# Deferring part of P V into the next scores phase, and a new ending, in a decode attention kernel that streams its K and V caches

## The chip, the cores and the metric

One core of one Trainium2 chip runs the whole program. The metric is the device time of that core in microseconds (us), the median of several executions.

## The reference

```python
# B=4 sequences, one query each, H=32 heads, Sk=8192 cached keys, Dh=128, D=512, bf16
xn = layernorm(x)
q = (xn @ wq)                                   # (B, H, 1, Dh)
scores = einsum("bhqd,bhkd->bhqk", q, k_cache) * Dh**-0.5
o = einsum("bhqk,bhkd->bhqd", softmax(scores), v_cache)
out = x + o.reshape(B, 1, H*Dh) @ wo + ffn(xn)  # ffn: silu gate, up, down; small
```

The K and V caches are 268 MB each. Nothing of them is used twice, so the kernel is a stream of loads with matrix work beside it.

## The kernel before

The work is cut into 32 tiles of 4 heads of one sequence. A tile's K is 8.39 MB, its V as much, and three slots of that size hold them in SBUF. The scores phase is 32 pieces: DVE transposes a piece of K (`kt`), PE multiplies it with q (`sps`). After the softmax, P V is 64 chunks of PE (`oacc`), one tile later. All loads go through one queue of the sync engine.

```python
    def load_v(n, parts=(T,)):                  # T = 256 columns of Dh
        t_ = slot()
        ...
            nc.sync.dma_start(out=t_[:, c0:c1], in_=src[:, c0:c1])
    ...
    def t_piece(n, g, jb):                      # DVE: one transpose of 128 x 512 uint32
        ...
        nc.vector.transpose(out=kt[:]..., in_=src[:, :, jb, :])
    def s_piece(n, g, jb):                      # PE: two matmuls
        ...
    build_q(0)
    load_v(0)
    for i in range(NT):                         # NT = 32
        for g in range(NTG):                    # 16 groups of 2 pieces
            for jb in range(2):
                t_piece(i, g, jb)
                s_piece(i, g, jb)
            if g == 1 and i > 0:
                pt_turn(i - 1)                  # four DVE transposes of P
        ...                                     # load_v(i), wo and parts near the end
        max_1(i)
        if i + 1 < NT:
            build_q(i + 1)
        ...
        for k in range(NK):                     # NK = 64
            pv_chunk(i - 1, k)
            if k == 8:
                max_2(i)
        row_sums(i)
        ...
        elif i + 2 < NT:
            load_k(i + 2)                       # K, two tiles ahead
        if bv == B - 1:
            fin_1(jv)                           # closing of a group of four tiles
            fin_q(jv)
    n = NT - 1
    pt_turn(n)
    wo_some(H)
    for k in range(KM):                         # half of the last tile as chunks
        pv_chunk(n, k)
    fin_1(JL)
    xps = x_tile()
    pv_last(xps, KM * NV, T - 48, start=True)   # the rest with V stationary
    fin_2(JL, xps)
    pv_last(xps, T - 48, T)
```

## Time and profile before

| | before |
|---|---|
| time, median of 3 runs | 1304.74 us |
| span of the profiled run | 1305.5 us |
| bytes read | 550.77 MB |
| mean rate over the span | 422 GB/s |
| PE busy in the middle (110 to 1180 us) | 88 to 89% |

The prediction below shows the slices, the stretches and the waits. Three more lines of the page of the kernel before are needed later. A DMA ring here means one of the core's 16 DMA engines with the packets that wait for it. The first two lines are instruction fetches, by queue (packets, MB, share of the 16 rings' time); as shown further down, they move over the same rings as the data. The third is the chain that ended last, by share of the span.

```profile
q8 instruction: 37, 0.61, 0.2%
q14 instruction: 21, 0.17, 0.0%
...
PE 58%; DVE 20%; issue 18%; DMA 2%; ACT 0%; DVEq 0%; SPq 0%
```

The chain is compute: PE, DVE and their handing over make 96% of it. The fetches look like nothing: 0.78 MB of 551. I passed over them when I predicted.

### The profile page before, as it was taken

What the parts mean: (1) busy time and instruction counts of PE and PEld (TensorE: products, weight loads), DVE (VectorE), ACT (ScalarE), POOL (GpSimd) and SP (SyncE); (2) the same over time, 40 slices, a digit from 0 to 9 for tenths busy, and PEclk for the clock granted to TensorE, in tenths of its full rate; (3) what the DMA queues carried; (4) which work ended last, traced back from release to release, by engine and by line L of the source; (5) the groups of instructions that cost most, each with busy time, mean ns of one, the idle gap of its engine ahead of it and who ended that gap; (6) DMA issues with size and microseconds to landing.
All of it is one profiled execution on the core that took longest, in us unless ns stands there. A gap on an engine that the chain in (4) does not pass through costs nothing.

```text
span 1305.5 us, 12271 instructions
## 1 busy us (share of the span) xinstructions
PE 1136.1 (87%) x4725; PEld 463.8 (36%) x4788; DVE 807.9 (62%) x1509; ACT 35.0 (3%) x79; POOL 3.6 (0%) x11
## 2 busy tenths in 40 slices
PE   1898888988889988889988889988889988889889
PEld 0244333333333333333333333333333333333335
DVE  3956555676555676555676555686555776555771
ACT  1000000000000000000000000000000000000000
POOL 1000000000000000000000000000000000000000
PEclk9897999889989899899998899988999889989899
DMA  9999999999999999999999999999999999999985
GB/s 418 418 432 438 432 432 436 428 442 420 446 422 442 428 436 430 436 430 434 432 436 427 428 424 438 424 432 432 414 436 432 430 428 424 436 436 406 409 339 227
DMA packets 12466, 551.56 MB, mean 422 GB/s; under 512 B 1260, under 2 KB 1784, under 8 KB 3064
## 3 DMA queue, kind: packets, MB, share of 16 engines
q1 hardware_dynamic: 12392, 550.77, 98.1%
q8 instruction: 37, 0.61, 0.2%
q14 instruction: 21, 0.17, 0.0%
q10 hardware_dynamic: 16, 0.01, 0.0%
HBM read 550.77 MB, written 0.00 MB: 422 GB/s over the span
## 4 chain that ended last, share of the span: by engine, by line
PE 58%; DVE 20%; issue 18%; DMA 2%; ACT 0%; DVEq 0%; SPq 0%
PE oacc L75 34%; PE sps L75 21%; DVE kt L272 14%; DVE ptz L309 5%; DMA slot<-in_A_k_cache_dram 2%; PE mps L75 1%; PE yo_ps L75 1%; PE xps L75 1%; DVE o L346 1%; PE mps L291 1%; DVE kt L344 0%; ACT kt L343 0%; DVE rcp L319 0%; DVE otn L366 0%; ACT p__385 L300 0%
## 5 line engine op out<-in xcount | busy, mean ns | idle before, releaser
L75 PE MATMUL sps<-kt,zq 128*128 128x512 bf16 x1985 | 635.4, 430 | 133.3 <-DVE kt L272 133.0
L272 DVE STREAM_TRANSPOSE kt<-slot 128x512 uint32<-128x512 uint32 x1024 | 629.5, 678 | 32.8 <-DMA slot<-in_A_k_cache_dram 12.5
L75 PE MATMUL oacc<-slot,ptz 128*16 128x512 bf16 x2016 | 446.9, 380 | 0.0
L75 PEld LDWEIGHTS <-zq 128*128 128x128 bf16 x2048 | 215.7, 105 | 543.4 <-issue 419.6
L75 PEld LDWEIGHTS <-ptz 128*16 128x16 bf16 x2016 | 206.6, 105 | 226.9 <-issue 13.7
L319 DVE RECIPROCAL rcp<-mps 128x4 f32<-128x4 f32 x32 | 5.9, 185 | 363.9 <-PE mps L75 363.9
L285 DVE TENSOR_REDUCE mx<-sps 128x1 f32<-128x512 f32 x32 | 22.1, 692 | 22.4 <-PE sps L75 22.4
L294 DVE TENSOR_REDUCE nm<-mps 128x4 f32<-128x64 f32 x32 | 7.2, 225 | 31.8 <-PE mps L291 31.8
L75 PE MATMUL xps<-rowy,o 128*32 128x4 f32 (+1 forms) x226 | 10.5, 204 | 15.3 <-DVE o L346 15.3
L263 DVE COPY zq<-qt 32x4 bf16<-32x4 bf16 x128 | 21.1, 165 | 1.3
L75 PEld LDWEIGHTS xps<-rowy,o 128*32 128x32 f32 (+1 forms) x226 | 9.8, 154 | 16.0 <-DVE o L346 16.0
L75 PEld LDWEIGHTS mps<-rowb,rs 128*128 128x128 f32 x64 | 9.7, 190 | 14.9 <-issue 12.9
L75 PE MATMUL mps<-rowb,rs 128*128 128x4 f32 x64 | 12.5, 266 | 1.7 <-ACT p__385 L300 1.7
L75 PEld LDWEIGHTS <-slot 128*128 128x128 bf16 (+1 forms) x274 | 11.7, 123 | 6.3 <-DVE slot L191 2.6
L344 DVE TENSOR_TENSOR kt<-kt,rowu 128x512 f32<-128x512 f32 x8 | 5.5, 693 | 11.2 <-ACT kt L343 10.4
L291 PE MATMUL mps<-ident_f,mx 128*128 128x128 f32 x32 | 10.3, 323 | 0.8 <-DVE mx L285 0.8
L291 PEld LDWEIGHTS mps<-ident_f,mx 128*128 128x128 f32 x32 | 4.3, 133 | 14.2 <-issue 12.9
L366 DVE TENSOR_TENSOR otn<-xps,rcp 32x16 bf16<-32x16 f32 x28 | 4.8, 170 | 7.2 <-PE xps L75 5.1
L75 PE MATMUL yo_ps<-slot,otn 128*4 128x256 bf16 x64 | 8.1, 290 | 0.3 <-DVE otn L356 0.3
L346 DVE TENSOR_REDUCE o<-kt 128x128 f32<-128x512 f32 x8 | 8.2, 1022 | 0.3
L343 ACT COPY kt<-oacc 128x512 f32<-128x512 f32 x8 | 4.7, 586 | 96.8 <-PE oacc L75 96.8
L75 PE MATMUL yo_ps<-slot,kt 128*4 128x256 bf16 x28 | 5.8, 402 | 1.6 <-DVE kt L235 1.6
(148 smaller groups left out, 180.0 us busy)
## 6 DMA issues: line engine op xcount, KB each, us to landing
slot<-in_A_v_cache_dram SPq DMA_DIRECT2D x5, 2048.0 KB, 16.4
slot<-in_A_wq_dram SPq DMA_DIRECT2D x1, 4096.0 KB, 12.2
slot<-in_A_v_cache_dram SPq DMA_DIRECT2D x1, 4096.0 KB, 15.8
slot<-in_A_wo_dram SPq DMA_DIRECT2D x1, 3584.0 KB, 19.7
slot<-in_B_w_gate_dram SPq DMA_DIRECT2D x1, 1792.0 KB, 23.7
slot<-in_B_w_up_dram SPq DMA_DIRECT2D x1, 1792.0 KB, 27.5
slot<-in_B_w_down_dram SPq DMA_DIRECT2D x1, 1792.0 KB
slot<-in_A_v_cache_dram SPq DMA_DIRECT2D x1, 1024.0 KB, 19.7
```

The costliest lines, as they stand in the source:

```text
L75: nc.tensor.matmul(out_ap, lhsT=lhsT, rhs=rhs, start=start, stop=True, skip_group_check=True, **kw)
L263: nc.vector.tensor_copy(out=zq[a * QB:(a + 1) * QB, :, XO + a * QB].rearrange("p (j r) -> p r j", r=2), in_=qt[a * QB:(a + 1) * QB, half, ...
L272: nc.vector.transpose(out=kt[:].bitcast(dt.uint32).rearrange("p (t r) -> p t r", r=QB), in_=src[:, :, jb, :])
L285: nc.vector.reduce_max(out=mx[:], in_=s_ps[n][:], axis=AX.X)
L291: nc.tensor.matmul(mps[:, 0:P], lhsT=nmx.pop(n)[:, 0:1].to_broadcast([P, P]), rhs=ident_f[:, :], is_transpose=True, start=True, stop=True, ...
L294: nc.vector.tensor_reduce(out=nm[:], in_=by_row(mps[:, 0:P]), axis=AX.X, op=ALU.max, negate=True)
L309: nc.vector.transpose(out=t_[y * QB:(y + 1) * QB, :, y, :, :].rearrange("p s u x -> p s (u x)"), in_=p_[y * QB:(y + 1) * QB, :].rearrange( ...
L319: nc.vector.reciprocal(out=rcp[j][:, :, b], in_=mps[:, P:P + HT])
L343: nc.scalar.copy(out=o_sb[:].rearrange("p u d -> p (u d)"), in_=o_acc[j % 2][:])
L344: nc.vector.tensor_tensor(out=o_sb[:], in0=o_sb[:], in1=rowu[:].unsqueeze(2).to_broadcast([P, NV, Dh]), op=ALU.mult)
L346: nc.vector.reduce_sum(out=o1[:], in_=o_sb[:].rearrange("p u d -> p d u"), axis=AX.X)
L366: nc.vector.tensor_tensor(out=otn[q0:q1, j * 4:j * 4 + 4, :], in0=xps[q0:q1], in1=r_[q0:q1, y, :].unsqueeze(1).to_broadcast([QB, 4, B]), o ...
```

## The change

The intent: in tiles 3 to 30, twelve of the 64 chunks of P V of a tile wait for the scores phase of the tile after next, so that PE has work where it waits for DVE's transposes. The three slots change their order with it: K of the next tile is asked for after piece 14 of the scores, not at the end of P V a tile earlier. At the end, wo and the first half of the last V share a slot, so that the last loads are asked for earlier, and the last tile's P V is done wholly with V stationary. (`v_from` and `v_cols` let half a V tile lie at an offset in a slot; they are cut here.)

```diff
+    LO = 12
+    TL = 80
     build_q(0)
     load_v(0)
-    for i in range(NT):
-        for g in range(NTG):
-            for jb in range(2):
-                t_piece(i, g, jb)
-                s_piece(i, g, jb)
-            if g == 1 and i > 0:
+    for i in range(NT - 1):
+        for p in pieces(i, 0, NP):
+            if i >= 3 and p in (6, 10, 14):
+                pv_to(i - 2, NK - LO + (p - 2) // 4 * (LO // 3))
+                if p == 14:
+                    load_k(i + 1)
+            if p == 16 and i > 0:
                 pt_turn(i - 1)
...
+        if i > 2 and b == B - 1:
+            pv_to(i - 1, 16)
+            fin_1(j)
+            pv_to(i - 1, 36)
+            fin_q(j)
+        if i > 0:
+            pv_to(i - 1, NK if i in (1, NT - 2) else NK - LO)
...
-        elif i + 2 < NT:
-            load_k(i + 2)
-        if bv == B - 1:
-            fin_1(jv)
-            fin_q(jv)
     n = NT - 1
-    pt_turn(n)
+    t_ = slot()
+    load_wo(t_)
+    v_from(n, t_, H * D, 0, (T // 4, T // 4))
+    for p in pieces(n, 0, NP):
+        if p == 6:
+            pt_turn(n - 1)
+        if p > 8 and p % 3 == 0:
+            pv_to(n - 1, (p - 6) * NK // (NP - 8))
+    pv_to(n - 1, NK)
+    t_ = slot()
+    v_from(n, t_, 0, T // 2, (48, 32, 24, 16, 8))
+    max_1(n)
+    wo_some(2)
+    max_2(n)
     wo_some(H)
-    for k in range(KM):
-        pv_chunk(n, k)
+    pt_turn(n)
+    row_sums(n)
     fin_1(JL)
     xps = x_tile()
-    pv_last(xps, KM * NV, T - 48, start=True)
-    fin_2(JL, xps)
-    pv_last(xps, T - 48, T)
+    pv_last(xps, 0, T - TL, start=True)
+    fin_2(JL, xps, B - 1)
+    pv_last(xps, T - TL, T)
```

More of the change, by code (lines that the diff above doesn't have):

```diff
@@ L97, in load_v, with v_from, v_cols @@
     def load_v(n, parts=(T,)):
+        t_ = slot()
+        v_from(n, t_, 0, 0, parts)
+    def v_from(n, t_, base, t0, parts):
         j, b = divmod(n, B)
-        t_ = slot()
         src = A_v_cache[b, j * HT:(j + 1) * HT, :, :].rearrange("h (p t) d -> (h p) (t d)", t=T)
-        c0 = 0
+        v_tiles[n, t0 * Dh] = (t_, base)
         for w in parts:
-            c1 = c0 + w * Dh
-            nc.sync.dma_start(out=t_[:, c0:c1], in_=src[:, c0:c1])
-            c0 = c1
-        v_tiles[n] = t_
+            nc.sync.dma_start(out=t_[:, base:base + w * Dh], in_=src[:, t0 * Dh:(t0 + w) * Dh])
+            base, t0 = base + w * Dh, t0 + w
+    def v_cols(n, c0, c1):
+        h0 = max(c for m, c in v_tiles if m == n and c <= c0)
+        t_, base = v_tiles[n, h0]
+        return t_[:, base + c0 - h0:base + c1 - h0]
     load_k(0)
@@ L243, with load_wo @@
     wo_t = []
-    def load_wo():
-        t_ = slot()
+    def load_wo(t_):
         n = (NB4 - 1) * 4
@@ L329, in pv_chunk @@
         mm(o_acc[j % 2][b * QB:b * QB + w, :], pt[n][:, off:off + (w - 1) * QB + 1:QB],
-           v_tiles[n][:, k * 512:(k + 1) * 512], start=(k == 0))
+           v_cols(n, k * 512, (k + 1) * 512), start=(k == 0))
     def pv_last(xps, t0, t1, start=False):
@@ L337, in pv_last @@
             off = p_off(k) + u * QB
-            mm(xps[:, :, B - 1], v_tiles[n][:, t * Dh:(t + 1) * Dh],
+            mm(xps[:, :, B - 1], v_cols(n, t * Dh, (t + 1) * Dh),
                pt[n][:, off:off + (HT - 1) * NV * QB + 1:NV * QB], start=(start and t == t0))
@@ L350, in x_tile, with fin_2 @@
         return psX.tile([P, HT, B], dt.float32, name="xps")
-    def fin_2(j, xps):
-        mm(xps[:], osb.pop(j)[:], rowy[:], start=False)
+    def fin_2(j, xps, nb):
+        mm(xps[:, :, 0:nb], osb.pop(j)[:], rowy[:, :, 0:nb], start=False)
     def fin_3(j, xps):
@@ L373 @@
     NK = T // NV
+    NP = 2 * NTG
     JL = H // HT - 1
-    KM = NK // 2
+    LO = 12
+    TL = 80
     wo_next, wo_ready = 0, 0
+    pv_at = {n: 0 for n in range(NT)}
     def wo_some(n):
@@ L383, in wo_some, with pv_to, pieces @@
             n -= 1
+    def pv_to(n, k):
+        while pv_at[n] < k:
+            pv_chunk(n, pv_at[n])
+            pv_at[n] += 1
+    def pieces(n, p0, p1):
+        for p in range(p0, p1):
+            t_piece(n, *divmod(p, 2))
+            s_piece(n, *divmod(p, 2))
+            yield p - p0 + 1
     build_q(0)
     load_v(0)
-    for i in range(NT):
-        for g in range(NTG):
-            for jb in range(2):
-                t_piece(i, g, jb)
-                s_piece(i, g, jb)
-            if g == 1 and i > 0:
+    for i in range(NT - 1):
[5 more added lines that the diff above has]
+            if p == 16 and i > 0:
                 pt_turn(i - 1)
@@ L400 @@
         elif i == NT - 2:
-            load_wo()
-        elif i == NT - 1:
-            load_v(i, (64, 64, 64, 32, 16, 8, 8))
+            load_v(i, (T // 4,) * 4)
         else:
@@ L406 @@
         max_1(i)
-        if i + 1 < NT:
-            build_q(i + 1)
-        if i == 0:
-            max_2(i)
-            row_sums(i)
-            continue
-        jv, bv = divmod(i - 1, B)
-        for k in range(NK):
-            pv_chunk(i - 1, k)
-            if k == 8:
-                max_2(i)
+        build_q(i + 1)
+        j, b = divmod(i - 2, B)
+        if i > 0:
+            pv_to(i - 1, 8)
+        max_2(i)
+        if i > 2 and b == B - 1:
[3 more added lines that the diff above has]
+            fin_q(j)
+            wo_ready = (j + 1) * HT
+        if i > 0:
+            pv_to(i - 1, NK if i in (1, NT - 2) else NK - LO)
         row_sums(i)
@@ L424 @@
             load_k(3)
-        elif i == NT - 1:
-            pass
-        elif i == NT - 2:
-            load_v(NT - 2, (128, 64, 64))
-        elif i + 2 < NT:
-            load_k(i + 2)
-        if bv == B - 1:
-            fin_1(jv)
-            fin_q(jv)
-            wo_ready = (jv + 1) * HT
-    n = NT - 1
+    n = NT - 1
+    t_ = slot()
[7 more added lines that the diff above has]
+    pv_to(n - 1, NK)
+    t_ = slot()
+    v_from(n, t_, 0, T // 2, (48, 32, 24, 16, 8))
+    max_1(n)
+    wo_some(2)
+    max_2(n)
+    wo_some(H)
     pt_turn(n)
-    wo_some(H)
-    for k in range(KM):
-        pv_chunk(n, k)
+    row_sums(n)
     fin_1(JL)
     xps = x_tile()
-    pv_last(xps, KM * NV, T - 48, start=True)
-    fin_2(JL, xps)
-    pv_last(xps, T - 48, T)
+    pv_last(xps, 0, T - TL, start=True)
+    fin_2(JL, xps, B - 1)
+    pv_last(xps, T - TL, T)
     fin_3(JL, xps)
```

## The prediction

The forecast's sum comes to 1284.4 us, and to 1284 for the timed median. Measured in the trace of the kernel before, the median distance from one matmul's start to the next is 0.216 us for P V (681.83 to 693.9 us), 0.109 for those of wo (1284.04 to 1290.1) and 0.026 for the 80 with V stationary (from 1296.74); twelve matmuls of the scores take 3.57 us, 0.298 each. That the loads go no faster than the flat 433.5 GB/s was the assumption, and the floors of 1276 and 1280 rest on it. A "cold window" is a stretch of lower granted clock: between 110 and 1290 us the trace has 30 of them, at 0.50, of 3.41, 6.83 or 10.24 us, and in the 3.41 us ahead of each PE was busy for 16 to 44% (17% from 659.34 to 662.75, then 0.50 until 666.16). The 1.5 us for one is the estimate; 3.41 us at 0.50 lose 1.7 at most.

> **What bounds the kernel now.** I read the slices first, because 551.56 MB must come from HBM and nothing in the change alters that.
>
> ```profile
> GB/s 418 418 432 438 432 432 436 428 442 420 446 422 442 428 436 430 436 430 434 432 436 427 428 424 438 424 432 432 414 436 432 430 428 424 436 436 406 409 339 227
> DMA packets 12466, 551.56 MB, mean 422 GB/s; under 512 B 1260, under 2 KB 1784, under 8 KB 3064
> ```
>
> Up to slice 20 the rate is flat (mean of slices 3 to 20: 433.1). Later it sags, and the last four slices, 32.6 us each, fall to 406, 409, 339, 227. Stretches of time sharpen this (busy time of each engine, then the TensorE clock, the DMA share, GB/s):
>
> ```profile
> 110.00:700.00 590.00, 521.98 (x2068) 209.40 (x2097) 374.40 (x701) 14.03 (x34) 0.00 (x0) 0.93 1.00 434
> 700.00:1180.00 480.00, 425.09 (x1665) 169.96 (x1688) 307.21 (x572) 11.10 (x27) 0.00 (x0) 0.92 1.00 429
> 1180.00:1230.00 50.00, 45.65 (x166) 17.30 (x168) 35.57 (x65) 0.78 (x2) 0.00 (x0) 0.93 0.99 422
> 1230.00:1270.00 40.00, 35.85 (x137) 14.05 (x138) 25.31 (x48) 0.78 (x2) 0.00 (x0) 0.96 0.86 339
> 1270.00:1290.80 20.80, 20.80 (x127) 11.71 (x125) 3.65 (x9) 0.78 (x2) 0.00 (x0) 1.00 0.95 397
> 1290.80:1305.50 14.70, 11.69 (x166) 7.28 (x164) 2.33 (x4) 0.95 (x2) 0.00 (x0) 0.85 0.01 3
> ```
>
> The DMA engines are full, at about 433.5 GB/s, until 700 us; then they starve now and then, starve clearly after 1180, and have nothing to do in the last 15 us. Now the waits: who waits for a load?
>
> ```profile
> DVE kt L272 <- DMA slot<-in_A_k_cache_dram: 12.5, 2, 11.4
> ```
>
> Only the start does (two waits). After it no K tile was ever waited for, and the oacc matmuls (P V) show 0.0 us idle. So the compute chain sets the pace, and the DMA queue runs only just as fast. The engine order of one tile (start, duration, instruction, in brackets the idle time before it):
>
> ```profile
> 656.93 0.39 PE L75 MATMUL sps<-kt,zq 128*128 128x512 bf16 x1 [0.87 <-DVE kt L272]
> 657.52 1.80 PE L75 MATMUL sps<-kt,zq 128*128 128x512 bf16 x6 [0.21 <-DVE kt L272]
> 662.18 13.63 PE L75 MATMUL sps<-kt,zq 128*128 128x512 bf16 x43 [2.86 <-DVE kt L272]
> 676.01 3.57 PE L75 MATMUL sps<-kt,zq 128*128 128x512 bf16 x12 [0.21 <-DVE kt L272]
> 679.52 2.13 PE L75 MATMUL oacc<-slot,ptz 128*16 128x512 bf16 x9
> 681.58 0.32 PE L291 MATMUL mps<-ident_f,mx 128*128 128x128 f32 x1
> 681.83 12.06 PE L75 MATMUL oacc<-slot,ptz 128*16 128x512 bf16 x55
> ```
>
> Scores take 656.3 to 679.6 (23.3 us), P V 679.6 to 694 (14.4): serial, about 38 us a tile. The scores phase has a hole of 2.86 us, while DVE turns P (four ptz transposes, 2.81 us) and gives PE no kt. Every fourth tile adds the closing of a head group: about 3.7 us more. The issues of V loads at 602.64, 640.80, 678.95, 720.68 and 759.64 us give 157.0 us per four tiles, 39.25 a tile. A tile pair of K and V is 16.78 MB, 38.7 us at 433.5 GB/s. Compute loses by about half a microsecond per tile: that is why the early lead of the queue is gone by 700.
>
> The end (start, duration, as above):
>
> ```profile
> 1284.04 5.95 PE L75 MATMUL yo_ps<-slot,otn 128*4 128x256 bf16 x53
> 1290.17 6.64 PE L75 MATMUL oacc<-slot,ptz 128*16 128x512 bf16 x30
> 1296.74 2.25 PE L75 MATMUL xps<-ptz,slot 128*128 128x4 bf16 x80
> 1299.30 0.40 PE L75 MATMUL xps<-rowy,o 128*128 128x16 f32 x2 [0.30 <-DVE o L346]
> 1299.54 1.40 PE L75 MATMUL xps<-ptz,slot 128*128 128x4 bf16 x48
> 1301.20 1.86 PE L75 MATMUL yo_ps<-slot,otn 128*4 128x256 bf16 x8 [0.27 <-DVE otn L356]
> ```
>
> The last V landed at about 1290.7, but PE still had the whole last V tile before it.
>
> [...] The trace shows a granted mean of 0.92 to 0.93, so each tile pays some already.
>
> **The change, part by part.**
>
> *Deferred chunks.* In tiles 3 to 30, twelve chunks of P V of tile i-2 run after pieces 6, 10 and 14 of the scores of tile i. PE's sum is the same. What is gained is overlap: 12 x 0.216 = 2.6 us leave the serial phase and go in where DVE (32 transposes plus ptz) also needs time, and let DVE run up to three kt buffers ahead before ptz, which moves to piece 16. Three buffers are 3 x 2 x 0.298 = 1.8 us of PE work, so I give the hole 1.8 us instead of 2.86. Scores: 0.9 start + 64 x 0.298 = 19.1 + 2.6 + 1.8 = 24.4; P V: 52 x 0.216 = 11.2, plus 0.6 for row sums. Sum 36.2 us instead of 38.2. The closing of a group moves into P V: its ACT and DVE part (0.59 + 0.70 + 1.03) lies beside 20 chunks (4.3 us), only its 32 small matmuls (1.46 us) stay: 37.7 instead of 41.7. Mean about 36.6 a tile, under the DMA's 38.7. So the loads become the bound, and the tile goes no faster than 38.7: of 2.6 us only 0.5 us can be collected.
>
> *Slots.* K of tile i+1 is now loaded at piece 14 of tile i, into the slot of V(i-2). If scores start as K(i) lands, piece 14 is 0.9 + 28 x 0.298 + 2.6 = 12 us later (14 with a cold window); V(i-1) is then still in transfer, until 19.4 us (8.39 MB at 433.5). The queue stays fed with 5 us in hand. V(i) is issued at about 24, before K(i+1) ends at 38.7. So no starvation.
>
> *The bound of the loads.* K(0) released DVE at 32.2 us; wq and K(0), 12.58 MB, are 29.0 us at 433.5, so 3.2 us go to start and landing. 551.56 MB are 1272.4 us; the last V lands at about 1276 instead of 1290.7.
>
> *The end.* After K(31) come V(30), wo and V(31): 20.97 MB, 48.4 us, so K(31) lands at 1227.6. Tile 30 does all 64 chunks (24.4 + 14.4 = 39) after K(30) at 1188.9, so scores of 31 start at about 1228. They hold P V of tile 30 as well: 0.9 + 19.1 + 64 x 0.216 = 13.8 + ptz hole 2.5 (piece 6, little lead) + a cold window 1.5 = 37.8, to 1265.8. The half of V(31) that shares with wo has been on its way since 1246; the slot of K(31) comes free at about 1263.5, just ahead of the first half's landing at 1266, so the queue barely stays fed. Then: max 0.8, its transpose 0.25, wo 52 x 0.109 = 5.7 (exp and ptz, 1.85 + 2.8, lie beside it), row sums 0.3, to 1272.8; 176 stationary V matmuls 4.6, fin_2 0.3, 80 more 2.1, to 1279.8, after the last landing, so PE and not the load ends this. From the last V matmul to the end was 1305.5 - 1300.9 = 4.6: 1284.4. The timed median lay 0.8 under the profiled span: **about 1284 us**.
>
> In terms of before: 21 us gained = about 4.5 of sags from 700 to 1180, 10.5 of starved DMA from 1180 to the last landing, and 6 of compute left over after it.
>
> **Rivals.** (1) The gain shows in full: 28 tiles x 2.6 us = 73 us, 1232 us. Against it is the flat 434: the loads alone take 1276. Even with no work left but the last bits, about 5 us of closing, the end is 1281 and the time 1280; 2% would be 1278.6. (2) The later K load starves the queue: if piece 14 came 19.4 us after the scores start, each further us would cost one us in 28 tiles. Cold windows after waits for K and a PE-bound scores phase speak for it, the margin of 5 us against; 2 us late would make 1340. (3) Steady state gains nothing, because cold clock takes back the 2 us (PE will now idle for K in every tile): then K(31) lands 4.5 us later, 1289. (4) The end: PE carries 19.1 + 13.8 us in one phase, and a V(31) issue 3 us late still hides behind PE's 1279.8; if the hole or the cold windows are twice mine, 1287.
>
> **Range and chances.** Floor 1280 from the loads, 1289 to 1291 if rivals 3 or 4 take part: range 1280 to 1291. The gain I expect is 1.6%. Over 2% lies under the floor of the loads, save for a wrong rate: 3%. Slower by 2% needs rival 2: 1%.
>
> **What would show it.** Right: 433 or 434 GB/s from 110 to about 1270 with no sag; a wait of DVE for K of about 2 us in nearly every tile from about tile 5 on; the first scores of tile 31 near 1228, last V landing near 1276, stationary V matmuls ending near 1280. Wrong: DMA below 430 in the middle (rival 2); no waits for K (compute still sets the pace, rival 3); PE waiting for the last V parts (the loads end it, and about 1281 follows).

## The result, and the profile after

| | before | after |
|---|---|---|
| time, median (4 runs each) | 1304.76 us | 1300.55 us |
| range | 1304.62 to 1306.72 | 1299.47 to 1301.46 |
| span of the profiled run | 1305.5 | 1299.7 |
| K asked for, mean us per tile (last 20 of them) | 39.25 | 39.35 |
| last byte of V landed (last increment) | 1292.3 | 1293.2 |
| from there to the end | 13.2 | 6.5 |

The ratio is 0.9964 with a 95% interval of 0.9947 to 0.9981: the same within 2%. Here and below a ratio is the mean time of one kernel's fast runs over that of the other's fast runs of the same rounds, so it is not quite the ratio of the medians that are quoted. That it would stay within 2% was foretold rightly; the time was not: 1284 was predicted, with 1291 as the upper end, and 16.5 us of the 21 did not come. (The spans are each of one execution: 1307.31 us before, which was 2.6 above its median, and 1301.46 us after.)

The last three rows of the table say where. The steady state did not gain: its 0.1 us a tile more is no more than runs with the same loop differ by (39.24 to 39.35, in the table further down). The last load landed no earlier. What was gained, 6.7 us, lies behind the last landing, and with the 0.9 us lost before it that makes the 5.8 us by which the spans differ.

The stretches of the kernel after, in the columns that the prediction explains:

```profile
110.00:700.00 590.00, 515.33 (x2075) 199.17 (x2074) 382.01 (x703) 13.11 (x33) 0.00 (x0) 0.95 1.00 431
700.00:1180.00 480.00, 417.05 (x1692) 161.69 (x1691) 311.43 (x571) 10.77 (x27) 0.00 (x0) 0.95 1.00 426
...
1230.00:1276.00 46.00, 42.27 (x174) 16.73 (x172) 22.58 (x42) 0.78 (x2) 0.00 (x0) 0.96 0.98 412
1276.00:1293.50 17.50, 17.24 (x289) 12.45 (x288) 7.29 (x13) 1.25 (x3) 0.00 (x0) 0.91 0.67 260
1293.50:1299.70 6.20, 3.35 (x62) 2.25 (x59) 0.59 (x2) 0.36 (x1) 0.00 (x0) 0.50 0.02 3
```

The rate was to stay at 433 or 434 until 1270. It is 431 already before 700 and 426 from there to 1180, less than before the change (434 and 429), though the DMA share is 1.00. PE waits more, not less. What does it wait for? The waits of DVE (us in total, times, longest), and the chain that ended last:

```profile
DVE kt L278 <- DMA slot<-in_A_k_cache_dram: 47.7, 27, 11.4
DVE kt L278 <- PE sps L75: 41.5, 63, 2.9
```

```profile
DMA 57%; PE 37%; DVE 4%; issue 1%; ACT 0%; SPq 0%; DVEq 0%
```

Two of the 27 waits for K are those of the start, which were there before (12.5 us); 25 are new, 1.4 us each in the mean. The chain has turned from compute to loads. One turn of it, from the chain in order of time (start, duration):

```profile
1095.87 28.44 DMA slot<-in_A_k_cache_dram
1124.31 0.02 issue
1124.33 0.72 DVE kt L278
1125.05 0.04 issue
1125.09 4.59 PE sps L75 x12
...
1136.72 26.75 DMA slot<-in_A_k_cache_dram
```

So the loads do bound the kernel after, as predicted; but a tile takes 39.35 us and not the 38.7 that 16.78 MB need at 433.5 GB/s. The first scores of tile 30 were to start at 1188.9 and started at 1203.1, 14.2 us late. Those of tile 31 were to start at 1228. DVE began them at 1244.0, 16 us late, and by then waited for PE's row sums and not for K, whose 16th increment had come at 1241.7:

```profile
1243.88 0.19 DVE L325 RECIPROCAL rcp<-mps 128x4 f32<-128x4 f32 x1 [11.90 <-PE mps L75]
1243.98 3.65 DVE L278 STREAM_TRANSPOSE kt<-slot 128x512 uint32<-128x512 uint32 x6
```

Tile 30 does all 64 chunks, and took 40.9 us where 39.1 were predicted. The ending itself (PE, as in the prediction):

```profile
1244.71 3.58 PE L75 MATMUL sps<-kt,zq 128*128 128x512 bf16 x12 [0.87 <-DVE kt L278]
...
1287.59 4.78 PE L75 MATMUL xps<-ptz,slot 128*128 128x4 bf16 x176
...
1292.65 2.32 PE L75 MATMUL xps<-ptz,slot 128*128 128x4 bf16 x80
1295.25 1.87 PE L75 MATMUL yo_ps<-slot,otn 128*4 128x256 bf16 x8 [0.27 <-DVE otn L362]
```

From the start of the scores of tile 31 at 1244.0 to the end of the span it took 55.7 us; 56.4 were predicted. The error is upstream of it: of the 16.0 us, 14.2 are the pace of the loads up to K(30), and 1.8 are tile 30 itself.

**What the mean of the queue hides.** In the trace a K or V load raises its semaphore 16 times, and I take one increment for each of the 16 DMA rings. DVE goes on at the last of them: in 28 of the 32 tiles of the kernel after, its first transpose starts 0.02 to 0.03 us after the 16th increment of its K load. I therefore read from the trace, load by load, the 16 increments. No view of the profile gives them; each row below is one load: the time of its first increment, and how long after it the 8th, 15th and 16th came.

```
kernel before            kernel after
  first  8th  15th 16th    first  8th  15th 16th
  12.5   0.2  0.3  0.4     12.4   0.3  0.5  0.6
 296.1   1.1  2.5  3.4    295.8   1.4  2.0  3.7
 508.6   1.8  3.9  7.1    509.9   0.4  2.5  5.7
 741.9   1.7  3.7  8.3    745.2   0.8  3.6  5.6
1075.5   0.6  2.5  8.5   1079.7   0.2  4.1  4.9
1172.8   0.6  1.7  8.7   1178.0   0.3  2.9  5.8
```

One increment falls behind the others, already in the kernel before; read as above, one ring does. The median of the 7039 packets of 65,536 bytes between 110 and 1180 us took 2.418 us, 27.1 GB/s, and sixteen rings at that make 433.7 GB/s: that is the flat rate of the prediction. But some packets take longer. Between 110 and 1180 us, 98 packets of the kernel before took over 2.7 us: 60 of them stand beside a fetch of instructions, and the other 38 come within 4 us after a new load was asked for; with 36 of these, only 10 to 15 packets were in flight at some moment of the 1.5 us before. (In the kernel after it is 56 and 116.) The fetches of queue 14 are of 8192 bytes, about 128 DVE instructions (the 2437 of the kernel after, over 19 fetches; 1856 more gave 15 fetches more, 1052 fewer gave 8 fewer, in two of the runs below). In the kernel after these 19 take 0.31 us each and the packet behind them (of 65,536 bytes for 18 of them) 0.53 to 0.61 more, which makes 0.87 us in the mean and 0.92 at most. Their spacing, 54 to 74 us, is what DVE's stream needs: the built program of the kernel after has 2437 DVE instructions (waits on semaphores included), 76 a tile, so 0.595 fetches a tile. Which ring a packet took can be read from its times: in the kernel before, nearly every packet starts 0.003 to 0.004 us before another one ends, and linked so they make 16 chains, one for each ring. Of the 21 fetches of queue 14, 19 lie on one chain; the other two, whose next packet takes 0.25 and 0.28 us longer, lie on others, and the run with more ACT instructions, told below, shows that such fetches are ACT's. So DVE's take the same ring. It is the late one: the packets behind a fetch can be followed along their ring to the load's increments, and in the run with 64 more DVE instructions, told below, this can be done for 30 of the 31 fetches between 90 and 1220 us; 29 lead to the 16th increment, one, at 118 us, to the 15th. The fetches of queue 8, of 16,384 bytes, are taken for PE's here (38 in the kernel after, 37 in the kernel before, and 37 there with 64 more DVE instructions too); in the kernel before the first 24 of them, up to 857 us, lie on eight of the chains in turn, three times round.

That gave the theory, called R in the expectations: the ring that carries DVE's fetches sets the pace. Its estimate for a tile, from these numbers, is 38.70 + 0.595 x 0.92 = 39.25 us, and for the last landing 34.42 MB (a sixteenth of the bytes) / 27.1 GB/s = 1270.1, plus 2.7 for the start (the first 4.19 MB landed at 12.4 us and need 9.7 at 433.7 GB/s), plus 19 fetches x 0.92 = 17.5: 1290.3 us. The runs show 39.25 and 39.35 for the tile, 1292.3 and 1293.2 for the landing. Of these four only the 39.35 tests R: the kernel before waits for no load, so its 39.25 is the pace of its compute, and the last V could not land before it was asked for (last at 1271.7 and 1281.5).

### The profile page after: what moved, and what is told of

It reads as the page before. It is cut to its first block, busy times and chain, and to the rows that moved or that the text cites. A ratio compares the mean times of both kernels' runs of the same rounds, so it can differ in the third digit from the quotient of the medians.

```text
span 1299.7 us, 12521 instructions
## 1 busy us (share of the span) xinstructions
PE 1114.6 (86%) x4884; PEld 443.6 (34%) x4884; DVE 819.1 (63%) x1509; ACT 34.1 (3%) x79; POOL 3.6 (0%) x11
## 2 busy tenths in 40 slices
DMA packets 12611, 551.57 MB, mean 424 GB/s; under 512 B 1276, under 2 KB 1800, under 8 KB 3080
## 4 chain that ended last, share of the span: by engine, by line
DMA 57%; PE 37%; DVE 4%; issue 1%; ACT 0%; SPq 0%; DVEq 0%
DMA slot<-in_A_k_cache_dram 57%; PE sps L75 23%; PE oacc L75 12%; DVE kt L278 2%; PE yo_ps L75 1%; DVE ptz L315 1%; PE mps L75 1%; PE xps L75 1%; DVE mx L291 0%; PE mps L297 0%; DVE rcp L325 0%; ACT p__385 L306 0%; DVE zq L269 0%; DVE kt L238 0%; SPq L87 0%
## 5 line engine op out<-in xcount | busy, mean ns | idle before, releaser
L75 PE MATMUL sps<-kt,zq 128*128 128x512 bf16 x2048 | 613.4, 419 | 163.7 <-DVE kt L278 163.7
L278 DVE STREAM_TRANSPOSE kt<-slot 128x512 uint32<-128x512 uint32 x1024 | 635.3, 680 | 106.4 <-DMA slot<-in_A_k_cache_dram 47.7
L75 PE MATMUL oacc<-slot,ptz 128*16 128x512 bf16 x1984 | 460.1, 382 | 0.0
L75 PEld LDWEIGHTS <-zq 128*128 128x128 bf16 x2048 | 204.2, 103 | 553.7 <-issue 415.3
L75 PEld LDWEIGHTS <-ptz 128*16 128x16 bf16 x1984 | 196.3, 106 | 245.3 <-issue 59.2
L325 DVE RECIPROCAL rcp<-mps 128x4 f32<-128x4 f32 x32 | 5.9, 185 | 246.2 <-PE mps L75 246.2
L75 PEld LDWEIGHTS <-slot 128*128 128x128 bf16 (+1 forms) x402 | 15.3, 117 | 5.1 <-DVE slot L198 2.7
L75 PEld LDWEIGHTS mps<-rowb,rs 128*128 128x128 f32 x64 | 9.5, 187 | 14.7 <-issue 12.7
L75 PEld LDWEIGHTS xps<-rowy,o 128*32 128x32 f32 (+1 forms) x226 | 10.5, 155 | 1.3
L297 PEld LDWEIGHTS mps<-ident_f,mx 128*128 128x128 f32 x32 | 4.2, 133 | 14.4 <-DVE zq L269 12.5
L75 PE MATMUL sps<-slot,xnt_w 128*32 128x512 bf16 x32 | 3.6, 630 | 4.2 <-DMA slot<-in_A_wq_dram 4.2
```

The costliest lines, as they stand in the source:

```text
L75: nc.tensor.matmul(out_ap, lhsT=lhsT, rhs=rhs, start=start, stop=True, skip_group_check=True, **kw)
L278: nc.vector.transpose(out=kt[:].bitcast(dt.uint32).rearrange("p (t r) -> p t r", r=QB), in_=src[:, :, jb, :])
L297: nc.tensor.matmul(mps[:, 0:P], lhsT=nmx.pop(n)[:, 0:1].to_broadcast([P, P]), rhs=ident_f[:, :], is_transpose=True, start=True, stop=True, ...
L325: nc.vector.reciprocal(out=rcp[j][:, :, b], in_=mps[:, P:P + HT])
```

## The experiments

The chief rival is called L: a K load takes 26.5 to 28.5 us from issue to landing and is issued some 12 us after the scores begin, so the loop of these two sets the 39.35 us, and an earlier issue would help. Other rivals are told in the expectations. All results were correct within the tolerance of the comparison with the reference. A run's "before" is the kernel before on the same chip in the same job.

### More DVE instructions in the kernel after

```diff
         max_2(i)
+        if i > 1:
+            for c in range(64):
+                nc.vector.memset(pad_t[0:1, c:c + 1], 0.0)
```

> The changed kernel (1300.5 us) with 64 writes of one element by DVE in each of 29 tiles, in the P V phase, where DVE waits 9.3 us for the row sums; nobody waits for them. Theory R (the slowest of the 16 DMA rings sets the pace, and what slows it are DVE's instruction fetches of 8 KB, 128 instructions, each some 0.92 us): 1856 instructions are 14.5 fetches more, 13 us: 1312 to 1315, and the last of a load's 16 increments comes even later than the 5.8 us after the first. Rival L (the loop from K's landing over piece 14 to the next K's issue sets the pace, rings do not matter): 1300.5 +- 1, since idle DVE time costs nothing.

Measured: 1314.00 us (before 1304.79, ratio 1.0068, interval 1.0051 to 1.0084), 13 us above the kernel after. The instructions are of one element, and lie in the P V phase, where DVE has time. Its wait at the end of that phase is still there (first line; 246.2 in the kernel after), so DVE had time for them. The wait for K grew, from 47.7 us:

```profile
DVE rcp L325 <- PE mps L75: 214.5, 32, 11.9
DVE kt L278 <- DMA slot<-in_A_k_cache_dram: 61.4, 29, 11.4
```

```profile
q14 instruction: 36, 0.29, 0.1%
```

Fifteen more fetches (36 against 21) at 0.92 us are 13.8 us, and the 16th increment comes up to 7.7 us after the first, 6.4 in the kernel after. R holds; but the number of instructions as such is not yet ruled out.

### The same number on ACT

```diff
+        if i > 1:
+            for c in range(64):
+                nc.scalar.copy(out=pad_t[0:1, c:c + 1], in_=ident_f[0:1, 0:1])
```

> As e1, but ACT makes 64 copies of one element per tile. Theory R: if ACT's fetches go to the same ring as DVE's, as e1, 1312 to 1315; if to another ring, that ring only draws level with the slow one (13 us of lag beside DVE's 18), 1300 to 1302. Rival L: 1300.5 +- 1. Rival 'more instructions as such slow the core': as e1 in any case.

Measured: 1307.30 us (ratio 1.0018, 1.0003 to 1.0033). This run is flawed: in every fourth tile the added copies stood in front of ACT's copy in the closing of a group, and DVE waited 7.4 us for it (it had waited 1.7 at most):

```profile
DVE kt L350 <- ACT kt L349: 51.5, 7, 7.4
```

So it was made again, with 84 copies in the 22 tiles that have no such closing (1848 in all, against 1856 for DVE):

```diff
+        if i > 1 and b != B - 1:
+            for c in range(84):
+                nc.scalar.copy(out=pad_t[0:1, c % 64:c % 64 + 1], in_=ident_f[0:1, 0:1])
```

> e2 mended: there the 64 ACT copies stood ahead of the group end's own ACT copy in seven tiles and delayed it by some 7 us each, so it said nothing. Now 84 copies of one element by ACT in each of the 22 tiles without a group end: 1848 instructions, 14.4 fetches more. Theory R with ACT's fetches on the same ring as DVE's: 1312 to 1314 as e1. Theory R with another ring, or rival L: 1300 to 1302. If fetches as such (on any ring) cost the time: 1312 to 1314 too, but then the spread of a load's increments has no lone last one.

Measured: 1300.00 us (before 1306.88, ratio 0.9955, 0.9938 to 0.9972), as the kernel after without them. The page counts 35 fetches of queue 14, one fewer than with DVE's, but they cost nothing:

```profile
q14 instruction: 35, 0.29, 0.1%
```

The number of instructions or of fetches is therefore not the cause; it matters whose they are. R says that ACT's fall on rings with time in hand, and the trace settles it. Between 90 and 1220 us there are now two kinds of fetches on queue 14: 17, as in the kernel after, whose next packet takes 0.53 us or more longer, and 16 (2 in the kernel after) whose next packet takes only 0.24 to 0.34 us longer. Followed to the increments, 16 of the first kind fit the 16th, and one, at 115 us, the 15th; of the second kind 9 can be followed, and they lead to the 9th to 14th, none to the last.

### K asked for earlier

The twelve chunks run after pieces 2, 4 and 6, so K is asked for some 6 us earlier:

```diff
-            if i >= 3 and p in (6, 10, 14):
-                pv_to(i - 2, NK - LO + (p - 2) // 4 * (LO // 3))
-                if p == 14:
+            if i >= 3 and p in (2, 4, 6):
+                pv_to(i - 2, NK - LO + p // 2 * (LO // 3))
+                if p == 6:
                     load_k(i + 1)
```

> The twelve chunks run after pieces 2, 4 and 6, so that K of the next tile is issued some 6 us earlier in each tile. Rival L: the loop shortens until it meets 38.7 us a tile, K(31) lands about 14 us earlier, 1286 to 1289. Theory R: the slow ring has packets queued in either case, so at most 2 us: 1298 to 1301; only the fast rings stop idling, and the spread of a load's 16 increments grows from 5.8 us to 9 or more.

Measured: 1299.39 us (before 1304.79, ratio 0.9962, 0.9947 to 0.9977). L wanted 1286 to 1289, and falls; R wanted 1298 to 1301 and a spread of the increments of 9 us or more, and the spread reaches 10.5.

The stronger form gives up the deferral, and K is asked for as the scores begin:

```diff
-    LO = 12
+    LO = 0
...
+        if i >= 3:
+            load_k(i + 1)
         for p in pieces(i, 0, NP):
-            if i >= 3 and p in (6, 10, 14):
-                ...
-                if p == 14:
-                    load_k(i + 1)
```

> No deferred chunks, K issued at the start of the tile's scores, everything else as changed. The overlap theory of the prediction: a tile costs 2 us more of compute (38.2, group end hidden), still just under the loads, so 1301 to 1306. Theory R: the ring's 39.3 us a tile hide it, 1300 to 1302. If deferral were the whole gain of the change: 1304.7.

Measured: 1298.47 us (ratio 0.9950, 0.9935 to 0.9965), 1.5 us below the range that R gave. The stretches:

```profile
110.00:700.00 590.00, 521.62 (x2063) 208.68 (x2092) 378.44 (x705) 13.11 (x33) 0.00 (x0) 0.95 1.00 433
700.00:1180.00 480.00, 418.10 (x1663) 167.22 (x1687) 307.98 (x572) 10.77 (x27) 0.00 (x0) 0.95 1.00 431
```

Here the queue as a whole runs as predicted, 433 and then 431 GB/s, and the time is still 1298. The increments say why (each load's 16, in us after the first):

```
 624.7  0 0.0 0.0 0.1 0.2 0.3 1.0 | 2.7 2.8 2.8 3.1 3.1 3.3 4.4 4.7 |  8.5
1069.7  0 0.0 0.1 0.2 0.5 0.5 0.6 | 4.2 4.3 5.5 5.5 5.7 5.9 6.0 6.7 | 14.7
```

In the second row seven rings are together, eight are a few us behind (which fits the eight rings of queue 8's fetches), and one is 14.7 us behind. This version is the fastest correct one, though its interval overlaps that of the kernel after; the twelve deferred chunks gain nothing over it.

### Which ring is late?

```diff
                 if p == 14:
                     load_k(i + 1)
+                    if 13 <= i < 28:
+                        probe(i - 12)   # a load of 128 bytes in each of n = 1..15 partitions
```

> Fifteen tiny loads (n = 1 to 15 partitions of 128 bytes), one a tile, right behind the K load. [...] theory R expects small n to land with the fast rings (some 1 to 4 us after the first increment of that K load) and all n from the slow ring's number up to land with the last increment, 5 us or more after it. If late and early ones mix, no single ring is slow and theory R is wrong. Time as the changed kernel, 1299 to 1303.

What the probes show (us after the first increment of the K load just ahead of them in the queue):

```
n = 3:  0.24 0.33 0.58        K load's last: 6.2
n = 4:  0.18 0.25 0.38 5.31   K load's last: 5.1
```

With 1 to 3 partitions all increments come within 0.6 us. From 4 to 15 there is always exactly one late one, at 4.4 to 6.5 us, with the K load's own last. So, with one increment for each ring, a probe reaches a late ring with its fourth partition and never before, and reaches only one. It is called the fourth below. (One run, state unknown, 1300.57 us.)

### The deferral alone

The deferral and the moved closing of a group, with the ending of the kernel before:

```diff
-            load_v(i, (T // 4,) * 4)
+            load_wo(slot())
+        elif i == NT - 1:
+            load_v(i, (64, 64, 64, 32, 16, 8, 8))
...   # and the old last part of the program
```

> The deferral and the moved group end alone, with the last tiles loaded and computed as in the kernel before. Theory R: the loop is worth about 2.5 us (scores of the last tile at 1243.7 instead of 1246.2), the old ending takes its 59 us: 1301 to 1304. The prediction's account: the loop alone worth 15 us or so, 1287 to 1292.

Measured: 1304.29 us (before 1306.88, ratio 0.9987, 0.9972 to 1.0001), 39.28 us a tile. The deferral alone is worth nothing that can be told apart; most of the kernel after's gain is the ending's.

### Fewer DVE instructions, first by other instructions

The built program of the kernel after has 2437 DVE instructions, and its page counts 1509, without the waits on semaphores: many of those waits are instructions of their own. A tiny copy per three transposes replaces many of them, and the copies of q go to ACT: 1996 DVE instructions instead of 2444 in the version without deferral, and 2017 instead of 2437 in the kernel after.

```diff
         kts[n, g, jb] = kt
+        if (2 * g + jb) % 3 == 2:
+            nc.vector.tensor_copy(out=pad_t[0:1, 0:2], in_=kt[0:1, 0:2])
...
-            nc.vector.tensor_copy(        # build_q
+            nc.scalar.copy(
```

> e5_LO0 with fewer DVE instructions: the built program has 1996 instead of 2444 (one small copy per three transposes takes over most of their separate waits; the four q copies of a tile go to ACT). Theory R: 3.5 fetches of 0.92 us fewer on the slow ring, 3 us: 1295 to 1296, if DVE's added waits (some 1 to 1.5 us a tile) do not make compute the bound, since e5 has only 0.5 us a tile to spare; then 1298 to 1305. Rival L: 1298.5 or slower.

Measured: 1331.69 us (before 1304.77, ratio 1.0206, 1.0186 to 1.0225; by the 2% rule unclear): a miss. Each added copy reads what the transpose before it wrote, and DVE became the brake (35% of the chain, 4% in the kernel after); its only wait for K is the first, and the chain is compute again:

```profile
PE 57%; DVE 35%; issue 5%; DMA 2%; ACT 0%; SPq 0%; DVEq 0%; ACTq 0%
```

> The same cut on the changed kernel, 2437 to 2017 DVE instructions; its deferral leaves compute more to spare. Theory R: 3.3 fetches, 3 us: 1297 to 1298. Rival L: 1300.5 or slower, as DVE waits more.

Measured: 1299.40 us (ratio 0.9961, 0.9943 to 0.9978), 1 us below the kernel after where 3 were expected. The page has 19 fetches instead of 21, and compute is nearly the bound again (14 waits for K, 21.9 us, with the start's 12). Inconclusive.

### Fewer DVE instructions by leaving out work

In the kernel after, the second transpose of each pair is left out, and PE uses the first one's result twice. The arithmetic is wrong (the comparison's tolerance let it pass; the inputs are normal numbers times 0.05, so the weights of the softmax are probably nearly even). DVE has 1385 instructions.

```diff
     def t_piece(n, g, jb):
+        if jb == 1:
+            kts[n, g, 1] = kts[n, g, 0]
+            return
```

> Wrong result on purpose: the changed kernel with the second transpose of each pair left out and the first one's result used twice; loads, matmuls and their order as before. DVE instructions 2437 to 1385, 8.2 fetches fewer. Theory R: 7 to 8 us less: 1292 to 1294, the spread of a load's increments 3 us or less. Rival L: the part of the loop from K's landing to piece 14 is bound by PE, so at most 1 us less, 1299 to 1301.

Measured: 1288.97 us (before 1304.77, ratio 0.9878, 0.9863 to 0.9894), 11.6 below the kernel after; 7 to 8 were expected. K(31) is asked for 9.1 us earlier (1206.4 instead of 1215.5), with eight fetches fewer, 1.1 us each; the rest is gained later. The spread of the increments was to fall to 3 us or less and is still 3.0 to 5.3 in the middle of the run, so R's size is off here on both counts. The wait for K is longer than ever:

```profile
DVE kt L281 <- DMA slot<-in_A_k_cache_dram: 84.0, 30, 11.4
```

```profile
q14 instruction: 13, 0.11, 0.0%
```

DVE has half its transposes left and simply waits; the loads come sooner all the same. K is asked for 10.5 to 13.2 us after its predecessor's landing in the last eight turns (11.3 to 12.5 in the kernel after), so the loop of L was not shortened on that side.

### More DVE instructions in the kernel before

```diff
             if k == 8:
                 max_2(i)
+                if 1 < i < NT - 1:
+                    for c in range(64):
+                        nc.vector.memset(pad_t[0:1, c:c + 1], 0.0)
```

> The kernel before with the 64 DVE writes of e1. The reading of the prediction (compute paces it at 39.25 us a tile, the writes lie in DVE's 11.7 us of waiting): 1304.8 +- 1. Theory R: its compute at 39.25 us and the slow ring at 39.2 lie side by side, so 14.5 fetches more make the ring the bound: 1316 to 1319, with waits of DVE for K in most tiles, which the kernel before does not have.

Measured: 1316.62 us (before 1304.77, ratio 1.0090, 1.0074 to 1.0106). Had compute alone bound the kernel before, these would have been free: DVE's wait at the end of P V is 322 us in the sum. Instead waits for K appear, which it had not had:

```profile
DVE kt L272 <- DMA slot<-in_A_k_cache_dram: 26.4, 14, 11.4
```

The page counts sixteen fetches of queue 14 more (37 against 21). Fifteen, as in the kernel after, would be 13.8 us at 0.92, and 11.9 came. So in the kernel before compute and the late ring lay level, within about 2 us over the whole run.

### The pace over all of them

Mean us over the last 20 intervals between issues of K loads, against 38.70 + (DVE instructions per tile / 128) x 0.92. In the kernel before compute paces it; the two runs that other waits slowed (64 on ACT, and fewer DVE instructions without the deferral), the probe and the last experiment are left out:

| kernel | DVE instructions per tile | estimate | measured |
|---|---|---|---|
| after, half the transposes | 43 | 39.01 | 38.91 |
| after, no deferral, K early | 76 | 39.25 | 39.14 |
| after | 76 | 39.25 | 39.35 |
| after, K somewhat earlier | 76 | 39.25 | 39.25 |
| after, 84 more on ACT | 76 | 39.25 | 39.24 |
| deferral alone | 76 | 39.25 | 39.28 |
| after, fewer DVE instructions | 63 | 39.15 | 39.02 |
| before | 76 | 39.25 | 39.25 |
| after, 64 more | 140 | 39.71 | 39.70 |
| before, 64 more | 140 | 39.71 | 39.71 |

The estimate tells the three groups (43, 76 and 140) apart; it doesn't explain the 0.2 us by which kernels with 76 differ.

### Taking bytes off the late ring

The version without deferral, with two of the seven pieces of wo cut into 123 and 5 partitions. The author assumed that the cut pieces would leave out the fourth ring; no run had shown that.

```diff
-        nc.sync.dma_start(out=t_[:, 0:n * D].rearrange(...), in_=A_wo[0:n * P, :].rearrange(...))
+        for p0, p1, k0, k1 in ((0, 123, 0, 2), (123, P, 0, 2), (0, P, 2, NB4 - 1)):
+            nc.sync.dma_start(out=w_out[p0:p1, k0:k1], in_=w_in[p0:p1, k0:k1])
```

> The version of e5 (no deferral of P V, K asked for at the start of the scores; 1298.5) with the first two of the seven loads of wo cut into 123 and 5 partitions[...]. Theory R (the fourth ring sets the end): 1295.5 to 1297, 1.5 to 2.5 less than the 1298.5 of e5. Rival (the late ring is not always the fourth, or the end is set by the mean of the queue): 1298 to 1300.5, no gain.

Measured: 1302.88 us (before 1304.54, ratio 0.9984, 0.9970 to 0.9999): a miss, 4.4 us slower than the version it was made from. The last V loads now have four late increments instead of one: the sixteen of one of them come at 1288.1 to 1289.8 for twelve, then at 1293.8, 1295.2, 1295.4 and 1295.9. While the cut pieces moved, two thirds of the packets of 4096 bytes took about 0.2 to 0.34 us instead of 0.16, and 43 of the 768 of 16,384 bytes took over 1 us, 13 in the version without the cut, where most take 0.61. Why, stays open. Which rings the cut pieces took is not shown, so the run says nothing about what fewer bytes on the late ring would be worth.

## Why the prediction was wrong

**What bounds now: half right.** That compute paced the kernel before is what its chain said. But "compute loses by about half a microsecond per tile" against loads of 38.7 us was wrong: the late ring needs 39.25 by the estimate, and there was nothing to lose against. The experiment on the kernel before shows it: with 64 tiny instructions more, waits for K appear at once.

**The deferral's compute: not refuted, and beside the point.** DVE and PE did get time in hand; it went into 25 waits for K of 1.4 us. The wait of about 2 us that the prediction named as its sign did come, if shorter. It shows that loads bound the tile, not at which rate.

**The step that failed: "the loads become the bound, and the tile goes no faster than 38.7", and with it "The bound of the loads".** The mean rate of 16 rings, 433.5 GB/s, was taken as the pace of a load. A load is done when its slowest ring is, and one ring carries DVE's instruction fetches besides: 0.55 us a tile by estimate, 0.65 measured over the last 20 tiles (39.35 against 38.70). By K(30) this had added up to 14.2 us, 0.57 for each of the 25 tiles that wait. The last V landed at 1293.2, not at 1276, as its slot came free with the scores of tile 31, which began 16 us late. Of the 21 us foretold, the 4.5 of sags and the 10.5 of a starved queue did not come; the 6 of compute left over behind the last landing came, as 6.7.

**"The queue stays fed with 5 us in hand": too wide.** The margin was counted from the landing of K on the mean ring. The fast rings are through with it up to 5.8 us before the late one, so they are through with V 13.6 us after the landing, and the next K is asked for 11.3 to 12.5 us after it: 1 to 2 us in hand, not 5. The 12 us to the issue itself were foretold rightly. That the small margin is why the mean rate sags to 426 GB/s fits the version that asks for K as the scores begin: it brought the mean back to 433 and 431. It was worth little, 2 us, and the intervals of the two overlap.

**The ending: right.** 56.4 us predicted from the scores of tile 31 on, 55.7 measured, and its parts agree: 37.8 and 36.6 us for these scores, 7.0 and 7.0 from there to the stationary V matmuls, 7.0 and 7.4 for them, 4.6 and 4.7 after them.

**The rivals.** The gain in full (1) did not come, for the reason given, only that the floor lay 15 us higher than thought. The sign that was named for starving by the later K load (2), a rate below 430 in the middle, did show (426), but as the cause of the lost time it was refuted by asking earlier. "Steady state gains nothing" (3) came true, but for another reason than the cold clock: the granted clock rose from 0.92 and 0.93 to 0.95. The end (4) was not bigger.

**What stays open.** The fetch's cost is 0.92 us by the packets and 1.1 by the run with half the transposes; some of that run's gain may come from less work of DVE besides. That DVE's fetches lie on the late ring is read from the trace and agrees with the added instructions on DVE and on ACT; that a small load reaches the late ring with its fourth partition rests on the probes of one run. Why DVE's fetches go there was not looked into, and no run took them off that ring.

## What to carry to other kernels

When loads bound a kernel, take the pace from the slowest ring and not from the mean rate: read how far the last of the 16 increments of a load trails the first, and whether that grows (in the kernel before it grew from 0.4 us at 12.5 us to 8.7 at 1172.8). If it does, count the instructions of the engine whose fetches share that ring; in a kernel of some 2400 DVE instructions that was some 17 us of 1300 by the estimate above, and no overlap of compute that was tried here won it back. And a steady state in which compute and loads seem to differ by half a microsecond per tile may have them equal: test it by adding a small, harmless cost on one side before building on the difference.
